# The second layer's low weights through TensorE and one PSUM bank, and the last short unit spread over the last tile's first layer

## The chip, the cores and the metric

The kernel runs on one core of a Trainium2 chip. Its time is the device time of one execution in microseconds (us). A kernel is timed in several runs, and its median counts. TensorE (PE) multiplies matrices, VectorE (DVE), ScalarE (ACT) and GpSimd (POOL) work element by element, and SyncE (SP) issues the DMAs. Matmul results land in PSUM, in banks of 128 x 512 fp32 numbers.

## The reference

Attention with a decay, and a feed-forward layer on its output:

```python
# q, k, v: (8, 8, 576, 64); f: (8, 8, 576); w_in: (512, 2048); w_out: (2048, 512), all fp32
scores = scale * np.matmul(q, k.transpose(0, 1, 3, 2))
cum = np.cumsum(np.log(np.clip(f, 0.0001, 1.0)), axis=-1)
scores = np.where(causal, -1000000000.0, scores + cum[:, :, :, None] - cum[:, :, None, :])
attn = softmax(scores); attn_out = attn @ v
x = attn_out.transpose(0, 2, 1, 3).reshape(4608, 512)
h = x @ w_in
g = h * np.clip(h + 3.0, 0.0, 6.0) / 6.0
out = g @ w_out
```

## The kernel before

The 64 heads are worked through one after the other. Batch 0 is done in two passes of another form (kinds A, four pairs of heads, and B, eight heads); the other 56 heads have kind F, the function `rows`: scores on TensorE, row maxima on VectorE (line 620), exponentials on ScalarE (line 632), the probabilities split into a high and a low fp16 part (lines 646 to 660), transposed by a DMA (line 667), and multiplied with v by `av` (lines 692 to 697).

Each number that enters a product of the feed-forward layer is held as a high and a low fp16 part, and a product is three matmuls (high x high, high x low, low x high). The tokens come in eight tiles of 512, one for each batch; the 64 tokens that are left of each batch are put together two batches at a time into short units of 128. A tile's first layer is 16 calls of `h_unit` (lines 768 to 787): twelve matmuls of 512 columns into one PSUM bank, a relu on ScalarE, a product on VectorE, and the split into the two halves of `gT`. Its second layer is four calls of `out_unit` (lines 815 to 831): 48 matmuls into one bank, a scaled copy on ScalarE and a DMA to the output. Tile 0 is done in two parts, the first 256 columns after kind A and the other 256 after kind B. A short unit's first layer is four calls of `h_short` (lines 789 to 813), each for four of the sixteen 128-column groups; the last short unit belongs to the last tile, writes its result into the buffer of v (`vst`), and has two `out_unit` calls of 256 columns each.

The PSUM banks of the feed-forward layer are handed out by `mm_tile` (lines 761 to 766): two banks in the pool `ps_m`, and, where its argument `three` is true, every third call takes the single bank of the pool `ps_t` instead. That bank also serves `pow2_scale` for v (line 182) and `max_rows` (line 499).

The weights arrive as fp32 in 16 chunks for each layer and are split by `w_split` (lines 282 to 295). The high part is a scaled fp16 copy on ScalarE (line 284). For the low part there are two ways: without the argument `eye`, VectorE computes x times scale minus high (line 295). With `eye`, minus the scale times the identity, TensorE multiplies that with x in fp32 (line 287) and adds high through the fp16 identity (line 288), and ScalarE copies the negated sum out of the bank (line 289). Three of the four column groups of the first layer's weights go through TensorE (`PE_LOW`, lines 314 to 319); the fourth and the whole second layer go over VectorE. The second layer's fp32 chunk k lies in row k + 1 of the buffer `w2` whose row k receives its fp16 parts (line 230): the high part of chunk k + 1 overwrites the fp32 numbers of chunk k.

The code gives an order of emission. The loop at its end walks through the heads; `fill` draws pieces of the feed-forward layer from a list of units by a credit that grows by a rate for each kind of head (lines 928 to 938), and `w_step` draws pieces of the weights' work. When the first layer of a part of tile 0 has been emitted, all that is left of the weights' work is emitted ahead of the output units (lines 841 to 843). The launch builds the program with `schedule_with_timeline_sim=True` (line 1071): the order in which the instructions stand on an engine is the scheduler's, and need not be that of the code. In the trace the last tile's four short steps are called ahead of all its output units, and the fourth one's matmuls end at 1064.8 us.

Of the kernel before, what the change touches and what calls it, by code (L numbers as in the profile page):

```python
# [9 lines left out]
F16 = mybir.dt.float16  # L10
BF16 = mybir.dt.bfloat16
F32 = mybir.dt.float32
# [3 lines left out]
ALU = mybir.AluOpType  # L16
# [4 lines left out]
def kernel(  # L21
# [10 lines left out]
    nc = tc.nc  # L32
# [3 lines left out]
    B = vS.shape[0]  # L36
# [3 lines left out]
    P = 128  # L40
# [5 lines left out]
    NFC = DFF // P  # L46
    TT = 512
# [7 lines left out]
    p2 = ctx.enter_context(tc.tile_pool(name="p2", bufs=2))  # L55
    ps_s = ctx.enter_context(tc.tile_pool(name="ps_s", bufs=2, space=bass.MemoryType.PSUM))
    ps_m = ctx.enter_context(tc.tile_pool(name="ps_m", bufs=2, space=bass.MemoryType.PSUM))
    ps_t = ctx.enter_context(tc.tile_pool(name="ps_t", bufs=1, space=bass.MemoryType.PSUM))
# [3 lines left out]
    identf = cpool.tile([P, P], F32, name="identf")  # L62
# [32 lines left out]
    QA = 256  # L95
# [35 lines left out]
    vst = cpool.tile([P, NCH, VR], F32, name="vst")  # L131
# [19 lines left out]
    NG = 4  # L151
    SC = cpool.tile([P, 80], F32, name="SC")
    SV, IV, UO, UX, A1 = 0, 8, 16, 24, 32
    S1, I1, S2, I2, S1R, I1R, SW2 = 64, 68, 72, 73, 74, 75, 76
# [46 lines left out]
    def scol(c):  # L201
        return SC[:, c:c + 1]
# [74 lines left out]
    def w_sum(a, b):  # L277
        pm = p2.tile([P, 1], F32, tag="pm", name=f"wm{a}")
        nc.vector.tensor_reduce(pm, wsum[:, a:b], axis=AX.X, op=ALU.add)
        return pm  # L280

    def w_split(i, k, sc, eye=None):
        _, x, (hi, lo) = w_chunk(i, k)
        nc.scalar.activation(hi, x, AF.Copy, scale=sc)
        if eye is not None:
            pl = ps_m.tile([P, TT], F32, tag="mm", name=f"low_{k}")
            nc.tensor.matmul(pl, eye, x, start=True, stop=False)
            nc.tensor.matmul(pl, ident16, hi, start=False, stop=True)
            nc.scalar.activation(lo, pl, AF.Copy, scale=-1.0)
            return  # L290
        if POOL_REST[i][k % 4]:
            nc.scalar.activation(x, x, AF.Copy, scale=sc)
            nc.gpsimd.tensor_tensor(lo, x, hi, op=ALU.subtract)
        else:
            nc.vector.scalar_tensor_tensor(lo, x, sc, hi, op0=ALU.mult, op1=ALU.subtract)  # L295
# [29 lines left out]
    def w_out_work():  # L325
        n = len(slots_out)
        for k in range(n):
            w_load(1, k, slots_out)
        yield

        for k in range(NW):
            w_decode(1, k, slots_out)
            if k + n < NW:
                w_load(1, k + n, slots_out)
            yield
        for _ in range(W_GAP):
            yield
        yield from pow2_scale(w_sum(NW, 2 * NW), S2, I2, "w1")
        nc.vector.tensor_reduce(scol(S1R), SC[:, S1:S1 + NG], axis=AX.X, op=ALU.min)
        nc.vector.tensor_reduce(scol(I1R), SC[:, I1:I1 + NG], axis=AX.X, op=ALU.max)  # L340
        nc.vector.tensor_scalar(
            SC[:, SW2:SW2 + NG], SC[:, I1:I1 + NG], scol(S1R), scol(S2),
            op0=ALU.mult, op1=ALU.mult,
        )
        for k in range(NW):
            w_split(1, k, scol(SW2 + k // NG))
            yield


# [411 lines left out]
    def mm_tile(name, three):  # L761

        turn[0] += 1
        if three and turn[0] % 3 == 0:
            return ps_t.tile([P, TT], F32, tag="tr", name=name)
        return ps_m.tile([P, TT], F32, tag="mm", name=name)

    def h_unit(t, fc, c0, c1):
        x = xT[t % 2]
        nw = c1 - c0  # L770
        ph = mm_tile(f"ph_{t}_{fc}_{c0}", t > 0 or c0 > 0)[:, :nw]
        fs_ = slice(fc * P, (fc + 1) * P)
        for cc in range(NCC):
            xh, xl = (x[:, cc, c0 // P:c1 // P, hl] for hl in range(2))
            nc.tensor.matmul(ph, w1[0][:, cc, fs_], xh, start=(cc == 0), stop=False)  # L775
            nc.tensor.matmul(ph, w1[0][:, cc, fs_], xl, start=False, stop=False)  # L776
            nc.tensor.matmul(ph, w1[1][:, cc, fs_], xh, start=False, stop=(cc == NCC - 1))  # L777
            if cc == 1 and nw == TT:
                yield H_COST
        r = p2.tile([P, TT], F32, tag="rt", name=f"r_{t}_{fc}_{c0}", bufs=3)[:, :nw]  # L780
        nc.scalar.activation(  # L781
            r, ph, AF.Relu, bias=bias_r, scale=scol(A1 + NG * t + fc * NG // NFC)
        )
        nc.vector.scalar_tensor_tensor(r, r, 6.0 * CG, ph, op0=ALU.min, op1=ALU.mult)  # L784
        nc.scalar.copy(gT[:, 0, fc, c0:c1], r)  # L785
        nc.vector.tensor_tensor(gT[:, 1, fc, c0:c1], r, gT[:, 0, fc, c0:c1], op=ALU.subtract)  # L786
        yield H_COST

    def h_short(u, j, gd):
        x = xS[u % 2]  # L790
        n = NFC // NG
        ph = mm_tile(f"phs_{u}_{j}", True).rearrange("p (f t) -> p f t", f=n)
        for i in range(n):
            fs_ = slice((n * j + i) * P, (n * j + i + 1) * P)
            for cc in range(NCC):
                xh, xl = (x[:, cc, :, hl] for hl in range(2))
                nc.tensor.matmul(ph[:, i], w1[0][:, cc, fs_], xh, start=(cc == 0), stop=False)
                nc.tensor.matmul(ph[:, i], w1[0][:, cc, fs_], xl, start=False, stop=False)
                nc.tensor.matmul(ph[:, i], w1[1][:, cc, fs_], xh, start=False, stop=(cc == NCC - 1))
            if i == 1:  # L800
                yield H_COST
        r = p2.tile([P, TT], F32, tag="rt", name=f"rs_{u}_{j}", bufs=3)
        r = r.rearrange("p (f t) -> p f t", f=n)
        for h in range(2):
            nc.scalar.activation(
                r[:, :, 64 * h:64 * h + 64], ph[:, :, 64 * h:64 * h + 64], AF.Relu, bias=bias_r,
                scale=scol(A1 + NG * (2 * u + h) + j),
            )
        nc.vector.scalar_tensor_tensor(r, r, 6.0 * CG, ph, op0=ALU.min, op1=ALU.mult)  # L809
        g = [gd[:, i, n * j:n * j + n, 0:P] for i in range(2)]  # L810
        nc.scalar.copy(g[0], r)
        nc.vector.tensor_tensor(g[1], r, g[0], op=ALU.subtract)
        yield H_COST

    def out_unit(s, three, col, rows_, gs=None, cols=(0, DM)):
        g = gT if gs is None else gs
        c = slice(*cols)
        po = mm_tile(f"po_{rows_[0]}_{cols[0]}", three)[:, c]
        ts_ = slice(s * P, (s + 1) * P)
        for fc in range(NFC):  # L820
            nc.tensor.matmul(po, g[:, 0, fc, ts_], w2[:, fc, 0, c], start=(fc == 0), stop=False)  # L821
            nc.tensor.matmul(po, g[:, 0, fc, ts_], w2[:, fc, 1, c], start=False, stop=False)  # L822
            nc.tensor.matmul(po, g[:, 1, fc, ts_], w2[:, fc, 0, c], start=False, stop=(fc == NFC - 1))  # L823
            if fc % 2 and fc < NFC - 1:
                yield 2.0 - H_COST
        o = p2.tile([P, DM], F32, tag="o", name=f"o_{rows_[0]}_{cols[0]}")
        nc.scalar.activation(o[:, c], po, AF.Copy, scale=scol(col))
        w = P // len(rows_)
        for i, r0 in enumerate(rows_):
            nc.sync.dma_start(out[r0:r0 + w, c], o[i * w:(i + 1) * w, c])  # L830
        yield 2.0 - H_COST

    def moe_tile(t, c0=0, c1=TT):
        for fc in range(NFC):
            j, new = divmod(fc, NFC // NG)
            if new == 0 and c0 == 0:
                while j not in w_in_done:
                    next(w_in_q, None)
                moe_scale_in(t, j)
            yield from h_unit(t, fc, c0, c1)  # L840
        if t == 0:
            for _ in wq:
                pass
        if c0 == 0:
            moe_scale_out(t)
        last = t == B - 1
        if last:
            gs = vst.bitcast(F16).rearrange("p c e -> p (c e)")[:, 0:2 * NFC * P]
            gs = gs.rearrange("p (a f t) -> p a f t", a=2, f=NFC)
            for j in range(NG):  # L850
                yield from h_short(t // 2, j, gs)
        r0 = t * S + (64 if t else 0)
        for s in range(c0 // P, c1 // P):
            yield from out_unit(s, t > 0 or s * P >= QA, UO + t, [r0 + s * P])
        if last:
            for cols in ((0, DM // 2), (DM // 2, DM)):
                yield from out_unit(0, True, UX + t, [(t - 1) * S, t * S], gs, cols)
# [82 lines left out]
    def one(*a):  # L940
        yield from moe_tile(*a)
# [19 lines left out]
    for i, (kind, n) in enumerate(VH):  # L961
# [29 lines left out]
        ph = next(sg)  # L991
# [83 lines left out]
```

## Time and profile before

| | us |
|---|---|
| median of three runs | 1076.95 |
| the three runs | 1076.81, 1076.95, 1079.76 |
| the profiled execution | 1080.35 |
| its span in the trace | 1078.6 |

The profile is of one execution. Busy time counts only the engine's own instructions. Idle time stands in square brackets or at a row's end, with what released the engine. A matmul's duration holds its way through the array; how fast matmuls follow each other is read from their starts. The granted clock is TensorE's, 1.0 at full speed.

### The profile page before, as it was taken

Reading aid. Unit: us, or ns where it says so; the run is one execution under the profiler, and the core shown is the slowest. Engines: PE = TensorE matmul, PEld = TensorE weight load, DVE = VectorE, ACT = ScalarE, POOL = GpSimd, SP = SyncE. Lnnn points to the kernel's source line nnn. Section 1 sums busy time; section 2 is a strip of 40 time slices with the busy share of each in tenths; the row PEclk is TensorE's granted clock in tenths of the full one; section 3 lists DMA queues with packets and bytes.
Section 4 is the critical chain, followed back from the end, with each engine's and each line's share of the span. In section 5 each row is a group of like instructions: output and inputs, shape, how many; then the busy total and the mean of one; then the engine's idle time right before and its main releaser. Section 6 shows DMA issues by size and latency. Waiting matters only on the chain.

```text
span 1078.6 us, 21257 instructions
## 1 busy us (share of the span) xinstructions
PE 1013.8 (94%) x7698; PEld 604.8 (56%) x7698; DVE 726.8 (67%) x1903; ACT 587.9 (55%) x1190; POOL 408.5 (38%) x505
## 2 busy tenths in 40 slices
PE   2799988899999999999999999999999999999897
PEld 2557854665455755555555755555555755544545
DVE  7887899887875668866865677767855678305300
ACT  4777657665664557555654547655743567315301
POOL 7434456454433445443434334443433442000000
PEclk9989989999999999999999999999999999999999
DMA  8976448965665676567465576567565554300000
GB/s 253 288 210 199 117 103 160 203 149 127 149 104 121 138 151 128 111 151 160 98 127 107 105 164 129 118 137 169 101 112 123 108 101 84 78 30 1 1 20 30
DMA packets 259300, 133.79 MB, mean 124 GB/s; under 512 B 226964, under 2 KB 228812, under 8 KB 259196
## 3 DMA queue, kind: packets, MB, share of 16 engines
q1 hardware_dynamic: 259196, 132.44, 55.7%
q8 instruction: 61, 1.00, 0.4%
q14 instruction: 43, 0.35, 0.1%
HBM read 47.93 MB, written 9.73 MB: 53 GB/s over the span
## 4 chain that ended last, share of the span: by engine, by line
PE 66%; DVE 13%; DMA 6%; ACT 6%; issue 5%; POOL 2%; SPq 1%; ACTq 0%; DVEq 0%; POOLq 0%
PE po L821 10%; PE po L822 10%; PE po L823 10%; PE ph L775 7%; PE ph L776 7%; PE ph L777 7%; DVE pp L620 3%; PE pn L609 3%; PE pn L612 3%; DMA vst<-in_vS_dram 2%; ACT pp L632 2%; DVE ring L649 2%; DVE gT L786 1%; DVE r L784 1%; DMA ring<-in_w_out_dram 1%
## 5 line engine op out<-in xcount | busy, mean ns | idle before, releaser
L632 ACT ACTIVATE pp<-pp,nb 128x192 f32<-128x192 f32 x280 | 138.9, 552 | 135.8 <-DVE nb L626 135.3
L821 PE MATMUL po<-w,gT 128*128 128x512 f16 x560 | 208.0, 383 | 5.2 <-DVE rs L809 2.8
L822 PE MATMUL po<-w,gT 128*128 128x512 f16 x560 | 210.2, 383 | 1.3 <-DVE w L295 1.3
L775 PE MATMUL ph<-xT,w 128*128 128x512 f16 (+1 forms) x576 | 201.5, 359 | 10.3 <-DVE r L784 10.1
L823 PE MATMUL po<-w,gT 128*128 128x512 f16 x560 | 210.1, 382 | 0.0
L776 PE MATMUL ph<-xT,w 128*128 128x512 f16 (+1 forms) x576 | 200.7, 358 | 0.0
L777 PE MATMUL ph<-xT,w 128*128 128x512 f16 (+1 forms) x576 | 200.0, 358 | 0.0
L649 DVE TENSOR_TENSOR ring<-pp,ring 128x128 f16<-128x128 f32 (+2 forms) x216 | 140.4, 660 | 82.6 <-ACT ring L646 81.6
L620 DVE CUSTOM_DVE_ANT_0 pp<-pn,W 128x192 f32<-128x192 f32 x280 | 123.3, 482 | 26.6 <-PE pn L612 25.0
L447 POOL TENSOR_SCALAR TK<-ST 64x576 fp32r<-64x576 f32 (+1 forms) x68 | 49.9, 733 | 240.8 <-PE pn L609 200.7
L459 POOL TENSOR_TENSOR T<-ST,T 64x576 fp32r<-64x576 f32 (+1 forms) x68 | 99.4, 1461 | 84.2 <-DMA T<-TK 72.5
L609 PE MATMUL pn<-TK,TQ 68*128 68x192 f32 x336 | 124.3, 384 | 5.0 <-issue 3.9
L784 DVE SCALAR_TENSOR_TENSOR r<-r,ph 128x512 f32<-128x512 f32 (+1 forms) x144 | 89.1, 620 | 56.2 <-ACT r L781 55.8
L785 ACT CAST gT<-r 128x512 f16<-128x512 f32 (+1 forms) x144 | 81.5, 568 | 80.8 <-DVE r L784 80.2
L786 DVE TENSOR_TENSOR gT<-r,gT 128x512 f16<-128x512 f32 (+1 forms) x144 | 103.9, 725 | 20.6 <-ACT gT L785 19.0
L781 ACT ACTIVATE r<-ph,bias_r,SC 128x512 f32<-128x512 f32 (+1 forms) x144 | 103.9, 725 | 23.1 <-PE ph L777 20.6
L646 ACT CAST ring<-pp 128x192 f16<-128x192 f32 x280 | 114.3, 449 | 0.0
L612 PE MATMUL pn<-T,T 128*128 128x192 f32 x336 | 113.0, 363 | 0.0
L456 POOL TENSOR_TENSOR T<-ST,TQ 64x576 fp32r<-64x576 f32 (+2 forms) x68 | 98.3, 1446 | 15.9 <-PE ps L552 5.4
L823 PEld LDWEIGHTS <-gT 128*128 128x128 f16 x560 | 55.0, 99 | 68.3 <-issue 9.2
L655 POOL TENSOR_TENSOR ring<-pp,ring 128x128 f16<-128x128 f32 x96 | 61.6, 642 | 80.5 <-ACT ring L646 35.2
L822 PEld LDWEIGHTS <-gT 128*128 128x128 f16 x560 | 54.9, 99 | 63.5 <-issue 8.5
(154 smaller groups left out, 1987.1 us busy)
## 6 DMA issues: line engine op xcount, KB each, us to landing
ST<-in_qk_dram SPq DMA_DIRECT2D x64, 288.0 KB
T<-TK SPq DMA_DIRECT2D x64, 144.0 KB
out_dram<-o SPq DMA_DIRECT2D x33, 256.0 KB
ring<-in_w_out_dram SPq DMA_DIRECT2D x16, 512.0 KB
T<-TQ SPq DMA_DIRECT2D x56, 144.0 KB
vst<-in_vS_dram SPq DMA_DIRECT2D x7, 1040.0 KB
ring<-in_w_in_dram SPq DMA_DIRECT2D x9, 512.0 KB
w<-in_w_in_dram SPq DMA_DIRECT2D x7, 512.0 KB
```

The costliest lines, as they stand in the source:

```text
L609: nc.tensor.matmul(dst, TQ[i][0:D + 4, qs], TK[i][0:D + 4, a:e], start=True, stop=False)
L612: nc.tensor.matmul(dst, T7[j][:, qs], T1[j][:, a:e], start=False, stop=True)
L620: nc.vector.tensor_tensor_reduce(pp[:r, w:w + kw], pn[:r, o:o + kw], W[:r, 4 * P + r - kw:4 * P + r], 1.0, -3.0e38, ALU.add, ALU.max, accu ...
L632: nc.scalar.activation(x_, x_, AF.Exp, bias=nb[:r, e0 + x:e0 + x + 1], scale=0.125)
L649: eng.tensor_tensor(hl[:r, a:a + c * P], pp[:r, at[c] + 64:at[c] + kw], hl[:r, h0[c] + 64:h0[c] + kw], op=ALU.subtract,)
L775: nc.tensor.matmul(ph, w1[0][:, cc, fs_], xh, start=(cc == 0), stop=False)
L776: nc.tensor.matmul(ph, w1[0][:, cc, fs_], xl, start=False, stop=False)
L777: nc.tensor.matmul(ph, w1[1][:, cc, fs_], xh, start=False, stop=(cc == NCC - 1))
L786: nc.vector.tensor_tensor(gT[:, 1, fc, c0:c1], r, gT[:, 0, fc, c0:c1], op=ALU.subtract)
L821: nc.tensor.matmul(po, g[:, 0, fc, ts_], w2[:, fc, 0, c], start=(fc == 0), stop=False)
L822: nc.tensor.matmul(po, g[:, 0, fc, ts_], w2[:, fc, 1, c], start=False, stop=False)
L823: nc.tensor.matmul(po, g[:, 1, fc, ts_], w2[:, fc, 0, c], start=False, stop=(fc == NFC - 1))
```

## The change

`w_split` gets its bank from `ps_t` for the second layer; `w_out_work` makes two scaled identities at a time in the buffer with the tag "junk" (one buffer) and passes one to each chunk. Tile 0 no longer asks for the third bank, in neither of its parts or layers. In the last tile, short step j is called after unit 4j + 1 of the first layer and no longer after all 16 units.

```diff
         nc.scalar.activation(hi, x, AF.Copy, scale=sc)
         if eye is not None:
-            pl = ps_m.tile([P, TT], F32, tag="mm", name=f"low_{k}")
+            pool, tag = (ps_t, "tr") if i else (ps_m, "mm")
+            pl = pool.tile([P, TT], F32, tag=tag, name=f"low_{i}_{k}")
...
         for k in range(NW):
-            w_split(1, k, scol(SW2 + k // NG))
+            j, new = divmod(k, NG)
+            if new == 0 and j % 2 == 0:
+                eyes = p2.tile([P, 2, P], F32, tag="junk", name=f"eyes{j}", bufs=1)
+                for i in range(2):
+                    nc.vector.tensor_scalar(
+                        eyes[:, i], identf, scol(SW2 + j + i), -1.0, op0=ALU.mult, op1=ALU.mult
+                    )
+            w_split(1, k, scol(SW2 + j), eyes[:, j % 2])
             yield
...
-        ph = mm_tile(f"ph_{t}_{fc}_{c0}", t > 0 or c0 > 0)[:, :nw]
+        ph = mm_tile(f"ph_{t}_{fc}_{c0}", t > 0)[:, :nw]
...
     def moe_tile(t, c0=0, c1=TT):
+        last = t == B - 1
+        if last:
+            gs = vst.bitcast(F16).rearrange("p c e -> p (c e)")[:, 0:2 * NFC * P]
+            gs = gs.rearrange("p (a f t) -> p a f t", a=2, f=NFC)
...
             yield from h_unit(t, fc, c0, c1)
+            if last and new == 1:
+                yield from h_short(t // 2, j, gs)
...
-        last = t == B - 1
-        if last:
-            gs = vst.bitcast(F16).rearrange("p c e -> p (c e)")[:, 0:2 * NFC * P]
-            gs = gs.rearrange("p (a f t) -> p a f t", a=2, f=NFC)
-            for j in range(NG):
-                yield from h_short(t // 2, j, gs)
         r0 = t * S + (64 if t else 0)
         for s in range(c0 // P, c1 // P):
-            yield from out_unit(s, t > 0 or s * P >= QA, UO + t, [r0 + s * P])
+            yield from out_unit(s, t > 0, UO + t, [r0 + s * P])
```

## The prediction

> **What bounds the kernel now.** I read the page's first part, then the busy time of each engine by stage, then the waits of the stages that the change touches, then single rows.
>
> ```profile
> PE 1013.8 (94%) x7698; PEld 604.8 (56%) x7698; DVE 726.8 (67%) x1903; ACT 587.9 (55%) x1190; POOL 408.5 (38%) x505
> ```
>
> TensorE (PE) is busy 94% of the span. The next view has seven columns after the stretch: its length, then PE, weight loads, VectorE (DVE), ScalarE (ACT) and GpSimd (POOL) with their instructions, then the granted clock.
>
> ```profile
> 0.00:136.00 136.00, 104.67 (x669) 81.22 (x670) 110.58 (x326) 90.90 (x190) 67.96 (x85) 0.96 0.72 212
> 136.00:194.00 58.00, 47.00 (x372) 29.74 (x373) 54.45 (x154) 37.85 (x82) 37.97 (x33) 0.91 0.68 133
> 194.00:204.00 10.00, 7.09 (x78) 5.39 (x77) 9.81 (x28) 7.70 (x19) 4.36 (x6) 0.93 1.16 280
> 204.00:324.00 120.00, 116.20 (x912) 70.61 (x911) 96.53 (x256) 75.79 (x160) 51.89 (x64) 0.98 0.67 135
> 324.00:1004.00 680.00, 673.92 (x5193) 378.42 (x5191) 448.25 (x1132) 364.40 (x725) 246.31 (x318) 1.00 0.55 113
> 1004.00:1079.00 75.00, 64.94 (x483) 39.37 (x480) 7.15 (x11) 11.25 (x21) 0.00 (x0) 0.96 0.06 18
> ```
>
> From 204 to 1004 us PE stands still only 3.8 + 6.1 = 9.9 us of 800. So time won or lost by PE before 204 us moves the end one for one, and so does time in the tail. The stage 136 to 194 is the one where the second layer's weights are split. There DVE is the bound (54.45 of 58 us), and PE stands 58 - 47.00 = 11.0 us at a clock of 0.91. What PE and ACT wait for there (total, times, longest), and what one split costs DVE:
>
> ```profile
> PE pn L609 <- issue: 3.9, 1, 3.9
> PE pav L692 <- DMA pT<-ring: 3.9, 4, 2.1
> PE po L821 <- ACT w L284: 1.8, 2, 1.4
> PE po L822 <- DVE w L295: 1.3, 3, 0.5
> ACT w L284 <- DVE w L295: 12.3, 5, 6.0
> 136.00:194.00 58.00, 14.58 (x16) 0.91 0.68 133
> 149.03 0.59 PE L821 MATMUL po<-w,gT 128*128 128x512 f16 x2 [1.37 <-ACT w L284]
> 153.56 0.50 PE L609 MATMUL pn<-TK,TQ 68*128 68x192 f32 x1 [3.94 <-issue]
> 155.26 0.64 PE L822 MATMUL po<-w,gT 128*128 128x512 f16 x1
> 155.69 0.63 PE L823 MATMUL po<-w,gT 128*128 128x512 f16 x1
> ```
>
> The sixth row is line 295 alone: 16 instructions, 14.58 us of DVE, a quarter of what fills it. ACT's high part of chunk k+1 overwrites the chunk that line 295 reads, so ACT waits 12.3 us for it. The long stop of PE (3.94 us) ends when DVE, far behind, has emptied a score bank. After it the same matmul starts every 0.43 us (155.26, 155.69) instead of every 0.22.
>
> **The low weights on TensorE.** *Removed:* 16 x line 295, 14.58 us of DVE. *Added on DVE:* four scaled identities, like line 317; on ACT: 16 copies out of the bank, like line 289; on PE: 16 chunks of two fp32 instructions and one fp16 instruction. The first layer does this already (twelve chunks), so every duration has a row:
>
> ```profile
> L317 DVE TENSOR_SCALAR eye<-identf,SC x3: 275/288/819, 30.8 to 71.5; 128x128 f32<-128x128 f32 x3
> L289 ACT ACTIVATE w<-low x12: 576/592/601, 39.6 to 83.4; 128x512 f16<-128x512 f32 x12
> 62.54 1.05 PE L287 MATMUL low<-gT,eye 128*128 128x512 f32 x2
> 63.43 0.38 PE L288 MATMUL low<-w,ident 128*128 128x512 f16 x1
> 63.65 1.02 PE L287 MATMUL low<-gT,eye 128*128 128x512 f32 x2
> 64.50 0.38 PE L288 MATMUL low<-w,ident 128*128 128x512 f16 x1
> ACT w L289 <- PE low L288: 1.3, 2, 0.9
> 54.00:96.00 42.00, 38.45 (x225) 27.32 (x225) 33.46 (x97) 32.33 (x69) 16.64 (x18) 0.90 0.70 209
> ```
>
> By starts, the fp32 pair takes 64.50 - 63.65 = 0.85 us and the fp16 one 63.65 - 63.43 = 0.22: 1.07 us a chunk, **+17.2 us of PE** for 16. DVE goes from 54.45 to 54.45 - 14.58 + 4 x 0.29 = 41.0 us, ACT from 37.85 to 37.85 + 16 x 0.592 = 47.3 of 58. DVE ceases to be the bound there, and PE becomes it.
>
> What PE gets back in the stage: the 3.9 us at the score bank, a wait on DVE's backlog; the 1.8 + 1.3 = 3.1 us for weights, whose cause, line 295, is gone; and of the 3.9 us for the transposed probabilities (a DMA behind DVE's and POOL's subtractions) half, 1.9, since only the DVE part gets earlier: 8.9 us. The clock: 0.09 x 58 = 5.2 us are lost, a part of it while PE stood anyway; with the standing gone I take 4.1 as returned. Its bounds are 0 and 5.2.
>
> What it adds in waits: each chunk now goes ACT (high), PE, ACT (low) through one bank. ACT waits for PE and behind it on ACT stand the softmax exponentials; PE's second matmul waits for ACT and behind it stand scores and output matmuls. The first layer's rows show 1.3 us of such ACT waits in 12 chunks with two banks; by that, 16 chunks cost 1.7. Bounds: nothing, if other matmuls stand between, and 16 x 0.592 = 9.5, if PE stands through every copy. I am nearer the low end, because the same stage has output and score matmuls to place between. One wait more is DVE's: the second pair of identities reuses the first pair's buffer and waits for chunk 7's matmuls, with the row maxima queued behind; it is once, and DVE has the room, so I take nothing, at most a chunk's 1.07.
>
> After the stage PE comes out later than the other engines. Its 2.9 + 3.8 = 6.7 us of standing from 194 to 324 are mostly such waits, and shrink; I take half, 3.4 (bounds 0 and 6.7).
>
> The bank rule: tile 0's second half loses the third bank, in both layers. Its cover is the attention's matmuls between the units.
>
> ```profile
> PE ph L775 <- DVE r L784: 4.7, 3, 2.0
> ```
>
> With three banks, PE waits 4.7 us in three waits from 194 to 324 for a bank. With two, sixteen 256-column units can wait more; without that cover a stop of the relu's and product's length could come at each. I take +1.0, one wait more of about the mean length (4.7 / 3 = 1.6), less cover. The bounds are -1 (the order also changes) and +5.
>
> Sum of this part: 17.2 + 1.7 - 8.9 - 4.1 - 3.4 + 1.0 = **+3.5 us**.
>
> **The last short unit.** The tail's rows:
>
> ```profile
> PE po L821 <- DVE rs L809: 4.6, 2, 2.8
> 1012.28 0.22 PE L799 MATMUL phs<-xS,w 128*128 128x128 f16 x1
> 1015.31 0.58 PE L821 MATMUL po<-w,gT 128*128 128x512 f16 x1 [2.80 <-DVE rs L809]
> 1015.69 0.63 PE L822 MATMUL po<-w,gT 128*128 128x512 f16 x1
> 1018.54 0.38 PE L823 MATMUL po<-w,gT 128*128 128x512 f16 x1
> 1018.76 0.38 PE L821 MATMUL po<-w,gT 128*128 128x512 f16 x1
> 1064.81 0.22 PE L799 MATMUL phs<-xS,w 128*128 128x128 f16 x1
> 1066.86 0.27 PE L821 MATMUL po<-w,vst 128*128 128x256 f16 x1 [1.83 <-DVE rs L809]
> ```
>
> Three of the four short steps end together at 1012.28 and hold all three banks until DVE's product: 2.80 us. The fourth ends at 1064.81, among the last output matmuls: 1.83 us more. Between 1015.69 and 1018.54 seven matmuls take 2.85 us that would take 7 x 0.22 = 1.5: 1.3 us of slow clock, and the first one some 0.2. With the four steps after units 1, 5, 9 and 13, two whole units follow the last of them before any output matmul wants its bank, and nothing is left for the end: **-6.1 us** (2.80 + 1.83 + 1.5).
>
> The cover inside the first layer:
>
> ```profile
> L781 ACT ACTIVATE r<-ph,bias_r,SC 128x512 f32<-128x512 f32 x16 | 12.3, 777 | 7.9 <-PE ph L777 7.9
> L805 ACT ACTIVATE rs<-phs,bias_r,SC 128x256 f32<-128x256 f32 x6 | 2.8, 568 | 5.9 <-PE phs L799 5.9
> L811 ACT CAST vst<-rs 128x512 f16<-128x512 f32 x3 | 1.8, 625 | 0.0
> ```
>
> A short step has 48 matmuls, 2.6 us of PE (a full unit: 12 x 0.22, the same), and 2 x 0.568 + 0.625 = 1.8 us of ACT, so ACT keeps up, and DVE does one product and one subtraction per unit as before. If that cover failed, the waits would stand earlier: up to 2.80 back. The DMAs are those of before, and none passes another queue's work; the buffer that the steps write (v's) has its last reader in an earlier split.
>
> The slow clock is where the Trainium skill can be weighed. The rows show half speed after a stop of 2.80 us. The Trainium skill's page "TensorE: Matmul & The Clock Gate", section "What's actually happening", says that the clock falls after at least one idle window of about 3.4 us; by it this stop would be too short, and the tail would gain 4.6, not 6.1. The trace disagrees, and decides.
>
> Total: 3.5 - 6.1 = -2.6 us. The profiled execution took 1080.35 us (span 1078.6), 3.4 above the median of the three runs, 1076.95; -2.6 on it is 1077.75. On the median it is **1074.35, say 1074.3 us**. The forecast's own range, with its inner bounds, is -6 to +1, 1071 to 1078.
>
> **The rivals.**
>
> *One bank stops PE (slower).* Place: between chunk k's fp16 matmul and chunk k+1's fp32 pair, 16 times. PE must wait until ACT has emptied the bank. Price: 0.592 us plus the way to ACT and back, up to 9.5 in all and, if the stops keep the clock low, the 4.1 us not returned: 9.5 - 1.7 + 4.1 = +11.9 on the forecast at worst, half of it, +6.0, as the typical case: **1080.3**. From 5.8 / 16 = 0.36 us of stop a chunk it decides (-2.6 becomes +3.2). For it: ACT at 47 of 58 us and strict chains. Against: the first layer, with its 1.3 us in all. The same page of the Trainium skill, section "A second HAM failure mode: psum-queue depth-cycling", describes this: short stops between groups of matmuls that turn through banks let the clock fall again and again. No run here shows it yet for one bank.
>
> *Two banks are too few for tile 0's second half.* +4 on the forecast: **1078.3**. For it: the 4.7 us that three banks already leave. Against: the first half ran on two banks, in a stage where PE had slack.
>
> *Everything fits into the gaps (faster).* All 11.0 us of standing, 4.1 of clock and 6.7 after the stage return: 17.2 - 21.8 = -4.6, and with the tail -10.7: **1066.2**. For it: PE had the gaps, and DVE gets 13 us. Against: the waits on the probabilities' DMA remain.
>
> *The change does not do what it says.* The order on an engine is not that of the code: the fourth short step stands at 1064.81 though the code calls it ahead of every output matmul. If the steps are pushed back to the end again, the tail keeps its 6.1 us: +3.5, **1080.4**.
>
> **How the numbers follow.** Chances: forecast 0.45, everything fits 0.20, two banks 0.15, one bank 0.13, not spread 0.07. What a measurement can tell from no change is about 0.3%, 3.2 us. The forecast lies at -2.6, so about half of its case (0.24) is faster by more than that and the rest the same; everything fits adds 0.20 to faster. Two banks go to the same, one bank to slower but for 0.01, not spread half to each. Faster 0.44, same 0.39, slower 0.17. The range takes in most of the fast rival and the two slow ones at their typical price: 1067 to 1081.
>
> **What would show it.** In the changed profile: today's line 295 with four instructions, 287 and 288 with 56 and 28; DVE near 41 us in the split's stage and PE near full there; a granted clock near 1.0; no wait of line 821 on line 809, and a full clock in the tail. It is wrong if PE's waits on ACT in the split pass 6 us, if tile 0's units wait for their banks more than 10 us, if the stage's clock stays at 0.91, or if line 797 still stands after 1010 us.

## The result, and the profile after

The change makes the kernel slower: 1136.95 us (median of four runs, 1135.69 to 1142.29) against 1077.73 us before (four runs, 1076.81 to 1079.76). The ratio is 1.0556, with a 95% interval of 1.0518 to 1.0594. The forecast was 1074.3 us, its range ended at 1081, and the direction was wrong too. The profiled execution took 1136.26 us, 1134.3 of them its span; before it was 1080.35 and 1078.6, so 55.7 us of span are to be found.

The page's first part, and the busy time by stage with the columns of before:

```profile
PE 1038.8 (92%) x7746; PEld 619.0 (55%) x7746; DVE 724.8 (64%) x1891; ACT 597.1 (53%) x1206; POOL 408.5 (36%) x505
```

```profile
0.00:136.00 136.00, 104.16 (x630) 77.79 (x631) 105.32 (x312) 90.34 (x188) 61.35 (x78) 0.97 0.66 197
136.00:194.00 58.00, 42.21 (x177) 19.96 (x175) 2.89 (x10) 19.78 (x33) 1.78 (x3) 1.00 0.07 19
194.00:204.00 10.00, 8.12 (x46) 7.08 (x46) 7.54 (x21) 3.00 (x5) 5.69 (x6) 0.76 0.54 171
204.00:324.00 120.00, 94.40 (x840) 68.05 (x840) 106.27 (x294) 71.55 (x163) 66.72 (x71) 0.89 0.77 153
324.00:1004.00 680.00, 671.61 (x5326) 382.35 (x5324) 476.01 (x1216) 379.47 (x766) 272.93 (x350) 1.00 0.59 123
```

In the stage of the split, 136 to 194 us, VectorE is busy for 2.89 of 58 us (before: 54.45) and GpSimd for 1.78 (37.97). Relief of 13 us was forecast for VectorE; in fact the attention stands still. PE is not idle meanwhile: it does the chunks and output matmuls. The loss shows later, from 204 to 324, where PE is busy for 94.40 us at a clock of 0.89 against 116.20 at 0.98.

An estimate sums this up: PE's busy time times the granted clock, as work at full speed. Before, the four stages to 324 us hold 100.5 + 42.8 + 6.6 + 113.9 = 263.8 us of work; after, 101.0 + 42.2 + 6.2 + 84.0 = 233.4. So 30.4 us less is done by then, and 17.2 us more have to be done for the chunks. From 324 to 1004 another 673.92 - 671.61 = 2.3 are lost. That is 50 of the 55.7 us; the clock's second digit alone is worth 1.2 us in a stage of 120.

What the engines wait for from 120 to 215 us (total, times, longest):

```profile
POOL TK L455 <- PE ps L557: 73.6, 1, 73.6
ACT w L284 <- PE low L288: 34.0, 15, 2.5
DVE junk L499 <- PE low L288: 28.9, 1, 28.9
DVE eyes L351 <- PE low L288: 25.0, 1, 25.0
...
PE po L830 <- ACT w L290: 15.3, 15, 1.1
```

Two waits of VectorE of 25 and 29 us end with chunks of the split, GpSimd waits 73.6 us for scores that PE gets to late (line 557 reads the buffer that GpSimd wants to fill), and PE waits 15 times about 1 us for ScalarE's copy. The timeline of one chunk, and of the end of the last (start, duration, engine, line; in brackets the idle time before it and what ended it):

```profile
156.60 0.38 PE L289 MATMUL low<-w,ident 128*128 128x512 f16 x1
...
156.81 0.48 DVE L351 TENSOR_SCALAR eyes<-identf,SC 128x128 f32<-128x128 f32 x2 [25.01 <-PE low L288]
...
157.49 0.58 ACT L290 ACTIVATE w<-low 128x512 f16<-128x512 f32 x1
158.12 0.38 PE L830 MATMUL po<-w,gT 128*128 128x512 f16 x1 [1.14 <-ACT w L290]
...
159.41 1.02 PE L288 MATMUL low<-w,eyes 128*128 128x512 f32 x2
...
160.27 0.38 PE L289 MATMUL low<-w,ident 128*128 128x512 f16 x1
...
186.14 0.69 DVE L499 CUSTOM_DVE_ANT_0 junk<-pn,W 128x512 bf16<-128x512 f32 x1 [28.85 <-PE low L288]
186.35 0.60 ACT L290 ACTIVATE w<-low 128x512 f16<-128x512 f32 x1 [2.62 <-PE low L289]
...
187.00 0.22 PE L508 MATMUL ptm<-identr,MC 128*3 128x128 f32 x1 [0.69 <-ACT w L290]
```

From one chunk's fp16 matmul to the next one's are 160.27 - 156.60 = 3.67 us: PE stops for the low part (1.14 us until 158.12), does six output matmuls with it (158.12 to 159.41), then the next chunk. ScalarE copies, PE goes on, VectorE and GpSimd hardly work. The single bank is free for another user only after the sixteenth copy, which starts at 186.35, and 187.00 is the first transpose of row maxima (`max_rows`, tile `ptm`) since 101.2 us. Where that leaves the attention, each line's first and last start (before, then after):

```profile
L500 PE MATMUL ptm<-identr,MC x12: 221/269/348, 17.7 to 120.6; 128*3 128x128 f32 x8, 128*4 128x128 f32 x4
L626 DVE TENSOR_SCALAR nb<-MF x112: 150/168/1376, 141.0 to 922.2; 128x3 f32<-128x3 f32 x56, 128x2 f32<-128x2 f32 x56
```

```profile
L508 PE MATMUL ptm<-identr,MC x12: 221/238/348, 18.3 to 188.4; 128*3 128x128 f32 x8, 128*4 128x128 f32 x4
L634 DVE TENSOR_SCALAR nb<-MF x112: 117/169/1376, 205.8 to 976.2; 128x3 f32<-128x3 f32 x56, 128x2 f32<-128x2 f32 x56
```

The last transpose of maxima of the batch-0 heads moves from 120.6 to 188.4 us, and the first bias of a kind-F head from 141.0 to 205.8, 64.8 us later. Some of that is caught up, and 54 us are left at the last head (922.2 to 976.2).

The tail, PE's waits near the end:

```profile
PE po L829 <- DVE r L792: 2.1, 1, 2.1
PE ph L783 <- DVE r L792: 2.1, 1, 2.1
PE po L829 <- ACT o L835: 0.8, 1, 0.8
```

The wait of 4.6 us for the short step's product is gone as forecast, and 5.0 us of other waits stand in its place.

### The profile page after: what moved, and what is told of

Read it like the earlier page. It is cut to its first block, busy times and chain, and to the rows that moved or that the text cites. A ratio compares the mean times of both kernels' runs of the same rounds, so it can differ in the third digit from the quotient of the medians.

```text
span 1134.3 us, 21362 instructions
## 1 busy us (share of the span) xinstructions
PE 1038.8 (92%) x7746; PEld 619.0 (55%) x7746; DVE 724.8 (64%) x1891; ACT 597.1 (53%) x1206; POOL 408.5 (36%) x505
## 4 chain that ended last, share of the span: by engine, by line
PE 71%; DVE 12%; ACT 6%; DMA 4%; issue 4%; POOL 2%; SPq 0%; ACTq 0%; POOLq 0%; DVEq 0%
PE po L830 10%; PE po L829 10%; PE po L831 10%; PE ph L783 7%; PE ph L785 7%; PE ph L784 7%; PE pn L617 3%; PE pn L620 3%; DVE pp L628 2%; PE low L288 2%; ACT pp L640 2%; DMA ring<-in_w_out_dram 2%; DVE ring L657 2%; PE pav L704 1%; PE pav L705 1%
## 5 line engine op out<-in xcount | busy, mean ns | idle before, releaser
L830 PE MATMUL po<-w,gT 128*128 128x512 f16 x560 | 208.5, 380 | 15.3 <-ACT w L290 15.3
L657 DVE TENSOR_TENSOR ring<-pp,ring 128x128 f16<-128x128 f32 (+2 forms) x216 | 144.1, 677 | 85.9 <-ACT ring L654 84.9
L467 POOL TENSOR_TENSOR T<-ST,T 64x576 fp32r<-64x576 f32 (+1 forms) x68 | 102.0, 1501 | 88.2 <-DMA T<-TK 78.0
```

Source lines behind the costliest of these rows:

```text
L657: eng.tensor_tensor(hl[:r, a:a + c * P], pp[:r, at[c] + 64:at[c] + kw], hl[:r, h0[c] + 64:h0[c] + kw], op=ALU.subtract,)
```

## The experiments

The first theory, from the two waits of VectorE, was the *shared buffer*: the identities share the one-buffer tag with the maxima, VectorE's queue stands behind them, and the attention with it. The rival, *bank order*: the single bank is handed out in the order of the code, so whatever comes behind the sixteen chunks there and needs that bank waits for all of them. Each version says what it is built on; times are medians, and ratios are to runs of the kernel before in the same comparison.

**Identities in a buffer of their own**, on the changed kernel.

```diff
-                eyes = p2.tile([P, 2, P], F32, tag="junk", name=f"eyes{j}", bufs=1)
+                eyes = p2.tile([P, 2, P], F32, tag="eyes", name=f"eyes{j}", bufs=2)
```

> The changed kernel, but the scaled identities lie in two buffers of their own and no longer in the single buffer that the row maxima of the batch-0 heads write to. Theory 'shared buffer': VectorE stood 25.0 + 28.9 us in order behind that buffer (second pair of identities, then the first row maximum), and the attention with it; with own buffers both waits are gone and the time falls to the 1077.7 us of before plus what the low weights cost net, 1074 to 1088 us. Rival 'one bank': ScalarE, TensorE and the bank in turn take 3.67 us a chunk and everything else waits for that; then the buffer changes little and the time stays above 1115 us. Rival 'order': the scheduler places the weights' work ahead of the attention; above 1115 us too, without a long wait of VectorE on TensorE.

1137.33 us, ratio 1.0544 (1.0515 to 1.0574): no gain. Its waits from 120 to 215 us:

```profile
POOL TK L455 <- PE ps L557: 74.9, 1, 74.9
DVE mr L510 <- PE ptm L508: 56.4, 1, 56.4
```

VectorE now gets past the identities and the maxima and stands for 56.4 us at the next step, for the transpose that needs the single bank. The shared buffer was a second lock beside the first. The theory falls.

**The maxima's scratch apart**, on the changed kernel: the same lock opened from the other side.

```diff
-            junk = p2.tile([P, S], BF16, tag="junk", name=f"junk_{v}_{c}", bufs=1)
+            junk = p2.tile([P, S], BF16, tag="junk2", name=f"junk_{v}_{c}", bufs=1)
```

> The changed kernel, but the row maxima of the batch-0 heads write their unused output to another buffer, while both pairs of identities still share one buffer. Theory 'shared buffer': the 28.9 us wait of the first row maximum goes, the second pair of identities still waits some 25 us for chunk 7, and VectorE's order holds back what stands behind it: about 1137 - 29 = 1108 us, between 1095 and 1120. Rivals 'one bank' and 'order': 1130 us and more.

1134.99 us in one run; VectorE waits 26.3 us for the identities and then 30.0 for the transpose. No gain either, against what was expected.

**The bank held without the low weights**, on the kernel before: each chunk still goes over VectorE, but takes the single bank once, for a two-column matmul and a two-column copy that nobody reads.

```diff
             w_split(1, k, scol(SW2 + k // NG))
+            pl = ps_t.tile([P, TT], F32, tag="tr", name=f"held_{k}")
+            nc.tensor.matmul(pl[:, 0:2], ident16, w2[:, k, 0, 0:2], start=True, stop=True)
+            held = p2.tile([P, 2], F32, tag="held", name=f"heldo_{k}", bufs=2)
+            nc.scalar.activation(held, pl[:, 0:2], AF.Copy, scale=1.0)
```

> The kernel before (low weights over VectorE), but after each of the second layer's 16 chunks a matmul of two columns on the chunk's high part goes into the single bank, and ScalarE copies these two columns out: the bank is taken and freed 16 times, with next to no work on any engine. Its result is used nowhere. Theory 'bank order': the single bank is handed out in the order of the code, so that the last two batch-0 heads' transposed row maxima, which come after the 16 chunks in the code, wait for all of them and with them all attention; then this kernel stops like the changed one, 1100 to 1145 us. Rival 'chain': the 47 us come from the work and the waits of the chunks themselves (fp32 matmuls, copies); then it stays within 10 us of before.

1100.74 us in one run, 24 over the median before (1076.59) and at the lower edge of what bank order expected, with almost no work added. Its waits from 120 to 215 us:

```profile
POOL TK L451 <- PE ps L553: 43.8, 1, 43.8
```

The last maxima's transposes stand at 156.5 and 158.1 us, behind the sixteenth chunk's high part at 154.3. Bank order is there, and costs about 24 us with next to no work behind it; ScalarE's 16 waits for the small matmuls, 11.7 us in all, are in that figure.

**The maxima moved off the bank**, on the changed kernel with identities of their own, and the same with the old bank rule and the old last tile as well (both as in the diff of the change, undone).

```diff
-        pt = ps_t.tile([P, 512], F32, tag="tr", name=f"ptm_{v}")
+        pt = ps_s.tile([P, 1024], F32, tag="S", name=f"ptm_{v}")
```

> The changed kernel with the identities in buffers of their own, and the transposed row maxima of the batch-0 heads in the banks of the scores and no longer in the single bank. Theory 'bank order': with neither buffer nor bank shared the attention goes on during the split; 1077.7 + 3.5 (low weights as forecast) + 9.5 (bank rule as measured alone) + 2 (spread as measured alone), about 1093 us, 1083 to 1103. Rival 'chain': above 1120 us.

> As the run before in this list, but with the bank rule and the last short unit as in the kernel before: only the low weights through TensorE and the single bank, without sharing. Theory 'bank order': the forecast's first part alone, +3.5 us, 1076 to 1088 us. Rival 'chain': above 1110 us.

1116.14 us in one run, and 1117.44 us, ratio 1.037 (1.0337 to 1.0403). Both expectations missed by 13 us or more. The second one's waits from 130 to 260 us name another user of the bank:

```profile
DVE e_v L187 <- PE pt_v L184: 23.5, 1, 23.5
```

This is the scale of the next batch's v (`pow2_scale`), for which VectorE stands 23.5 us.

**Low weights through two banks**, on the changed kernel with identities of their own, the old bank rule and the old last tile. The chunks take turns in the pool `ps_m`; maxima and v's scale stay in the single bank.

```diff
-            pool, tag = (ps_t, "tr") if i else (ps_m, "mm")
+            pool, tag = ps_m, "mm"
```

> The kernel before with only the low weights through TensorE, but through the two banks that the first layer uses, with own buffers for the identities; row maxima stay in the single bank, bank rule and short unit as before. Theory 'bank order': no head waits for a chunk; the output units, which come after the chunks in the code, get their banks later, so 1078 to 1092 us. Rival 'chain': the chunks' own waits stay, above 1110 us.

1088.68 us, ratio 1.012 (1.0083 to 1.0157), inside the expectation. From 136 to 194 us:

```profile
136.00:194.00 58.00, 46.46 (x314) 26.99 (x313) 40.77 (x139) 45.69 (x98) 29.08 (x30) 1.00 0.66 140
```

Here stands what the prediction had worked out for two engines of this stage: VectorE at 40.8 (forecast 41.0), ScalarE at 45.7 (47.3), and the clock at 1.00. TensorE was forecast near full, and stands for 58 - 46.46 = 11.5 us. And the kernel is still 1.2% slower. The two traces show only a part of that: the profiled execution took 1084.74 us, 4.4 more than the profiled one before.

**All other users moved off the bank.** Three versions: the low weights through the single bank with the maxima and v's scale in the scores' banks (old bank rule, old last tile); the change as it is with the same two moves; and as a control the kernel before with the two moves alone.

```diff
-        pool, tag = (ps_t, "tr") if SV < s_col < SV + B else (ps_m, "mm")
-        pt = pool.tile([P, 512], F32, tag=tag, name=f"pt_{name}")
+        if SV < s_col < SV + B:
+            pt = ps_s.tile([P, 1024], F32, tag="S", name=f"pt_{name}")
+        else:
+            pt = ps_m.tile([P, 512], F32, tag="mm", name=f"pt_{name}")
```

> Low weights from TensorE through the single bank, with identities in a buffer of their own, the old rule of banks and the old last tile; the row maxima's transposes and the scale of v both move to the scores' banks, so that until tile 0's outputs only the chunks use the single bank. Bank order (what comes behind the chunks in the code and needs the single bank waits for all of them): no stop of attention is left, and the time is that of the version with two banks, 1088.7 us, give or take the slower chunks: 1082 to 1096. The rival, that the chunks themselves are too slow by the single bank (3.67 us each, in turn with the outputs) and hold the attention through the order of TensorE's queue: 1105 to 1120, as with the maxima moved alone (1117.4).

> The change as it is, with identities in a buffer of their own and both the maxima's transposes and the scale of v in the scores' banks. Bank order, with costs that add up: the version before it in this call plus 7 to 12 us for the rule of banks in tile 0 and plus 0 to 3 us for the spread unit, 1090 to 1108. The rival (the bank rule costs something only while attention isn't held up, or the chunks are the hold-up): 1112 to 1120, as with the maxima moved alone (1116.1).

> Control: the kernel before with the maxima's transposes and the scale of v in the scores' banks, nothing else. If moving them is neutral, as both theories take it, 1075 to 1081; if the scores' banks are themselves short, 1082 to 1095, and what the two kernels with moved users lose is partly the move.

1115.46 us (ratio 1.0364, 1.0338 to 1.039), 1120.18 us (1.0416, 1.0388 to 1.0444) and 1085.67 us (1.0092, 1.0056 to 1.0127). The rival of the first run was right about the time: with no other user of the bank before tile 0's second half, it stays where it was. Yet the lock itself is gone: the last transpose of maxima stands at 129.9 us and the first bias of a kind-F head at 151.5 (control: 153.9). The control isn't neutral either. So bank order isn't all of it.

**Two banks again, in two surroundings:** with the two moves of the version of 1115.46 us, and in the change as it is with identities of their own. The edit is the one of the two banks above.

> Low weights through two banks, and the maxima's transposes and v's scale moved to the scores' banks as in the version of 1115.5; old bank rule, old last tile. If the single bank's pace cost the rest in that version (TensorE and ScalarE in turn, 16 times), this is near the sum of the two parts alone, 1.012 and 1.0092: 1095 to 1104. If it was the moved users together with the added work, in whichever bank: 1108 to 1118.

> The change with one thing undone: the low weights use the two banks of the other pool (identities in a buffer of their own); the bank rule of tile 0 and the spread short unit stay. Bank order, with costs that add up: 1.012 (low weights, two banks) plus 0.0088 (bank rule) plus 0.002 (spread) on 1076.6, so 1095 to 1105, and TensorE busy near 46 of 58 us from 136 to 194 with the last two maxima's transposes ahead of 125 us. The rival, that the loss is not the single bank's but the work that TensorE gained: above 1115, near the change's 1137.

1091.91 us (ratio 1.0111, 1.0078 to 1.0145) and 1105.5 us (1.023, 1.0205 to 1.0255). The first is below both expectations, nearer to that of the pace; the second is half a microsecond over the range of costs that add up. Between the first and the version with one bank, otherwise alike, stand 1.0364 - 1.0111 = 2.5%, 27 us by the ratios (23.6 between the medians). The first and last start of ScalarE's high part of the second layer's chunks shows a difference of pace, with one bank and then with two:

```profile
L286 ACT ACTIVATE w<-w,SC x16: 706/722/725, 135.2 to 226.7; 128x512 f16<-128x512 f32 x16
```

```profile
L286 ACT ACTIVATE w<-w,SC x16: 705/716/722, 132.9 to 186.0; 128x512 f16<-128x512 f32 x16
```

A chunk every 91.5 / 15 = 6.1 us with one bank, every 53.1 / 15 = 3.5 with two. A chunk goes through PE's queue and then ScalarE's, with the attention's work in both, before the bank is free. With one bank one chunk is on that way at a time, with two there are two. The outputs of tile 0's first half read all chunks. With one bank the last of these matmuls starts at 237.84 us, and the first layer of the second half at 238.27. With two the last one starts at 209.86; one of the second half's sixteen units stands ahead of it, and the others start at 210.08. So what PE could do between the attention's steps comes 28 us later, and PE does less from 204 to 324 us, with one bank and with two:

```profile
204.00:324.00 120.00, 105.58 (x776) 66.69 (x775) 79.89 (x221) 68.11 (x146) 48.31 (x57) 0.93 0.66 136
```

```profile
204.00:324.00 120.00, 115.61 (x967) 73.08 (x966) 96.84 (x266) 76.71 (x164) 53.00 (x64) 0.99 0.64 136
```

The change itself has another loss. There the attention stands still, and the chunks come with one bank at (182.5 - 130.9) / 15 = 3.4 us each, as fast as with two; the first layer of tile 0's second half starts at 188.45 us. So its loss is not the pace but the held attention. With two banks in the change that hold is gone: the last transpose of maxima stands at 120.2 us and the first bias of a kind-F head at 140.5, as before.

```profile
L508 PE MATMUL ptm<-identr,MC x12: 222/270/348, 17.6 to 120.2; 128*3 128x128 f32 x8, 128*4 128x128 f32 x4
```

By the ratios two banks bring 1.0544 - 1.023 = 3.1% back there, 34 us (against the version with identities of their own and one bank, otherwise alike; 31.8 between the medians). What is left agrees with the sum of three parts measured alone: 1.012 for the low weights, 1.0088 for the bank rule and 1.002 for the spread (both below) make 1.0228, measured 1.023. Not all costs add up so: 1.012 and the control's 1.0092 would make 1.0212, and together they gave 1.0111. Nor is the full clock from 136 to 194 us the two banks' doing: in this version it was 0.85.

**Half the dose:** the change with identities of their own, and only the first eight chunks on PE through the single bank.

```diff
-            w_split(1, k, scol(SW2 + j), eyes[:, j % 2])
+            w_split(1, k, scol(SW2 + j), eyes[:, j % 2] if k < 8 else None)
```

> A dose: the change with identities in a buffer of their own, and only chunks 0 to 7 through the single bank; chunks 8 to 15 over VectorE as before. Bank order: attention is held for about half of the 16 chunks' 58 us, 25 to 35 us, and the time is 1100 to 1115. The rival, a stop that does not depend on the chunks' number (a missing transfer, the identities): VectorE's long wait stays above 50 us and the time stays at 1130 to 1140.

1111.05 us, ratio 1.0291 (1.0261 to 1.0321), the time that bank order expected. From 120 to 215 us:

```profile
POOL TK L455 <- PE ps L557: 46.0, 2, 45.3
```

The stop goes with the number of chunks: 45.3 us for eight, 74.9 for sixteen. The first bias of a kind-F head comes at 180.1 us, 39.1 later than before, over the 25 to 35 that were expected. The time doesn't go in proportion: over the version with two banks, eight chunks cost 0.6% and sixteen 3.1%. The two are not quite alike, since that version has all sixteen chunks on PE; with half of the low weights' 1.2% taken off it, eight chunks would cost 1.2%, by this estimate. Either fits a stock of output matmuls which bridges the first part of the stop for PE and is then used up; it was not measured by itself.

**The bank rule alone**, on the kernel before.

```diff
-        ph = mm_tile(f"ph_{t}_{fc}_{c0}", t > 0 or c0 > 0)[:, :nw]
+        ph = mm_tile(f"ph_{t}_{fc}_{c0}", t > 0)[:, :nw]
...
-            yield from out_unit(s, t > 0 or s * P >= QA, UO + t, [r0 + s * P])
+            yield from out_unit(s, t > 0, UO + t, [r0 + s * P])
```

> The kernel before, with only the bank rule changed: tile 0's second half gets two banks instead of three. Theory 'shared buffer' gives this rule no share in the 59 us: 1077.7 within 4 us. Rival 'two banks': the rule costs a large part, over 1090 us.

1088.18 us, ratio 1.0088 (1.0064 to 1.0111): 7 to 12 us, well over the bounds. From 204 to 324 us, and PE's waits for a bank from 194 to 324:

```profile
204.00:324.00 120.00, 109.26 (x883) 67.81 (x880) 94.11 (x241) 72.72 (x153) 48.00 (x58) 0.96 0.65 136
```

```profile
PE ph L775 <- DVE r L784: 2.2, 1, 2.2
```

PE waits less at the banks, not more: 2.2 us in place of 4.7. It waits for the attention instead: 5.9 us for the transposed probabilities (1.0 before), 2.7 for the maxima (0.3) and 2.1 for GpSimd (none). It gets less done: 109.26 x 0.96 = 104.9 us of work at full speed against 113.9, 9.0 us less, about the whole loss. From 194 to 324 us the trace has 112 output matmuls where the one before has 153; 41 at 0.22 us make about the same 9.0.

**The spread short unit alone**, on the kernel before.

```diff
             yield from h_unit(t, fc, c0, c1)
+            if last and new == 1:
+                yield from h_short(t // 2, j, gs)
...
-            for j in range(NG):
-                yield from h_short(t // 2, j, gs)
```

> The kernel before, with only the last short unit's steps spread among the last tile's first layer. By the forecast's step the tail loses 2.80 + 1.83 us of stops and 1.5 us of slow clock: 1077.7 - 6.1 = 1071.6 us. By the trace of the changed kernel, whose tail has stops of 2.1, 2.1 and 0.9 us in other places and an end that waits for an output DMA, the stops only move: 1075 to 1080 us.

1080.32 us (ten runs), ratio 1.002 (0.9993 to 1.0047): no difference, where -6.1 us were forecast. The end of the last tile's first layer:

```profile
1013.00 0.22 PE L799 MATMUL phs<-xS,w 128*128 128x128 f16 x1
1015.33 0.38 PE L821 MATMUL po<-w,gT 128*128 128x512 f16 x1 [2.10 <-DVE r L784]
```

**A quarter with two banks**, to see whether any share pays: only the first four chunks on PE, through two banks, old bank rule, old last tile.

```diff
-            w_split(1, k, scol(SW2 + j), eyes[:, j % 2])
+            w_split(1, k, scol(SW2 + j), eyes[:, j % 2] if k < 4 else None)
```

> A dose with two banks: only the first four chunks of the second layer through TensorE, old bank rule, old last tile. A quarter of 1.012's loss is +3 us, a quarter of the forecast's gain is nothing: 1074 to 1082. If giving VectorE a little room is worth more than 4 x 1.07 us of TensorE: 1068 to 1074, which would beat both kernels.

1083.59 us (ten runs), ratio 1.0037 (1.0014 to 1.006): slightly slower than before. No version tried beats the kernel before.

## Why the prediction was wrong

*The step that failed* is the one with the added waits of the low weights. It costed the bank as a matter between PE and ScalarE ("by that, 16 chunks cost 1.7", bounds 0 to 9.5) and of VectorE's wait it said "it is once, and DVE has the room, so I take nothing, at most a chunk's 1.07". The waits came as foreseen in kind, but larger: PE waited 15 times, 15.3 us in all, over the bound; VectorE waited for the identities once, 25.0 us. (The bound took a stop as the copy alone, 0.592 us. In the timeline the copy is 0.58 of the 1.14; it starts 0.51 us after the end of the matmul before it.) But most of the price lay with neither. No term asked who else uses the single bank. `max_rows` and `pow2_scale` do, both behind the chunks in the code; the transposes of maxima that should have come by 120.6 us came at 187.0 and 188.4, and the attention with them. One bank instead of two costs some 34 us of the 59.2 here. That the order by itself stops the attention is shown (24 us with an almost empty matmul and copy per chunk, in one run), and that it isn't all: with the other users moved, one bank still costs 27 us over two, now with a pace of 6.1 us a chunk against 3.5. In these versions with one bank either the attention stands and the chunks go fast, or the attention goes on and the chunks are slow.

*The rival "One bank stops PE"* named the right resource and the wrong victim: it priced stops of PE at 9.5 us and 4.1 of clock at most, and ended at 1080.3. Its clock part didn't come: with 15 stops of 1.1 us the granted clock from 136 to 194 us was 1.00. The rule of the Trainium skill cited there, on micro-idling between groups that turn through PSUM banks, is not seen in this stage, where the groups turn through one bank. Nearer to the case is the Trainium skill's page "Perfetto Trace Analysis", section "Matmuls", which says that independent groups should rotate through different banks, so that the copy out of one overlaps the matmuls of the next. The 3.5 and 6.1 us a chunk agree with it; the 3.4 us with one bank, where the attention stood, do not show it.

*The work moved to PE* was wrong in its returns. With the low weights through two banks and nothing else of the change, VectorE's and ScalarE's busy times in the stage came out as worked out, but the time was 1.2% (12.1 us between the medians) over, where 17.2 + 1.7 - 8.9 - 4.1 - 3.4 = +2.5 was the sum. PE's standing of 11.0 us in the stage was not there to be had: it is 11.5 with two banks (58 - 46.46), and 10.2 and 11.2 in the other two versions with two banks. By these rows the 8.9 us "got back" are the term that was mis-sized; since the two profiled executions are only 4.4 us apart, the traces don't show all of the 12. The prediction took named waits as removable one by one; PE came to stand at others.

*The bank rule*: +1.0 forecast, bounds -1 to +5, measured 7 to 12. The bounds were made of waits at the banks, and those fell. The loss lies in PE getting less done from 204 to 324 us, with waits for the attention in their place. The rival "Two banks are too few" had the sign right, with +5 for the rule, but its cause, waits at the banks, isn't seen.

*The last short unit*: -6.1 forecast, no difference measured. The waits named did vanish, but not the slow clock: from 1015 to 1020 us it is 0.66 in the spread version, as before. And the step "two whole units follow the last of them before any output matmul wants its bank" failed: by that trace the last short step's matmuls end at 1013.00, and the first output matmul is the next, at 1015.33, after a stop of 2.10 us. The scheduler had taken units and short steps in groups and set the last one at the end, in the changed kernel as well. A second stop of 2.1 us stands within the layer and one of 0.8 near the end. The rival that the change does not do what it says was right about the cause, for this part of the change.

*A small slip:* by the chances that the prediction lists, same comes to 0.405 and slower to 0.155, not 0.39 and 0.17. Nothing hangs on it.

*What stays open.* How much of the 34 us a lock without the slow pace would cost can't be told cleanly: each edit lets the scheduler set a new order on every engine, and the control with two moves, meant to be neutral, cost 0.9%. That the late start of tile 0's second half is what costs the 27 us is read from the traces and was not varied by itself. Emitting the maxima and v's scale ahead of the chunks in the code was not tried.

## What to carry to other kernels

Before giving work to a buffer that exists once, list everyone else who takes it and where they stand in the code: most of the price of a lock was paid here by what came behind the last taker, not by the engines that work in it. Read a stage's standing engines together: a bound engine whose busy time falls to 5%, as VectorE's did, meant that its input had stopped, and the loss showed only later, from 204 us on. And a wait that is named in a profile is not time to be won until it is shown what the engine would do instead.

## What the runs showed that was not expected

One bank was enough to hold back 64.8 us of attention although PE stayed busy for 42.2 of 58 us and at full clock. Costs that were measured apart added up closely once, 1.0228 from three parts against 1.023, and another time they did not, 1.0212 against 1.0111. And moving two small matmuls to the scores' banks cost 0.92% (0.56 to 1.27%).
